# Fourier and mixture-of-experts kernel: sums of the right operands formed by adding DMAs, elementwise work moved from GpSimd to VectorE in the Fourier stage, one gate multiplied later

## The chip, the cores and the metric

One core of a Trainium2 chip runs the whole program. The metric is the device time of one execution in microseconds (us). Times of the profile come from one profiled execution, counted from its first instruction. PE is TensorE, PEld its weight loads, DVE is VectorE, ACT is ScalarE, POOL is GpSimd, SP is SyncE, which here only issues DMAs.

## The reference

For x of 2048 positions by 512 features, the output is g * a + (1 - g) * b, with one sigmoid gate g for each position:

```python
a_re = x @ dft_hid_re.T ; a_im = x @ dft_hid_im.T          # 512 x 512
a = dft_seq_re @ a_re - dft_seq_im @ a_im                  # 2048 x 2048
for e in range(8):                                         # all 8 experts, K = 8
    b += softmax(x @ w_gate)[:, e] * (silu(x @ w1[e]) @ w2[e])
g = sigmoid((x * gate_w).sum(-1))
out = g * a + (1 - g) * b
```

## The kernel before

Every large product is float32 made of two parts (a high part that ACT writes as fp32r, a low part that an elementwise engine gets by subtracting it), so one product of tiles is three matmuls (`mm`, lines 126 to 131). The products are arranged in blocks of 2 x 2 in a scheme of Strassen and Winograd with seven block products m = 1 to 7 in place of eight. It needs sums of blocks of each operand before the products and sums of products after them.

The program runs in this order. Stage 1 (`plan_stage1`) makes x times the hidden matrices, in two halves of positions (hf 0 and 1), seven products of 24 matmuls each, in the order `ORDER1`; `plan_x_op`, `plan_x_sums`, `plan_w_op`, `plan_w_sums` make its operands and `evict1` takes its results out of PSUM. Then come four phases of the sequence transform, in this order: X of output half 0, X of half 1, Y of half 1, Y of half 0 (below X0, X1, Y1, Y0). An X phase makes products 1, 2 and 5, a Y phase products 6, 3, 7 and 4, each over 16 steps k of the contraction (`dft`). One step is 18 matmuls of 512 columns in X and 24 in Y. The left operands of a step (tiles `xl`) are made once for both halves from the results of stage 1 (`raw`): for X by `plan_left_x`, for Y by `plan_left_y`, which loads the raw tile again from DRAM (`rawy`). The right operands are made anew in each step by `plan_right`: SP loads blocks of the sequence matrix (`cT`, tiles `ca`, `cb`, `cd`), sums are formed, and `wide` and `split_at` make the high and low parts (tiles c_kh, c_kl, from the pool `cp` of 9 buffers; the loads go to the pool `stage` of 6). In X one sum is made, d - a0, on DVE. In Y the first sum, b1 - b0, is made on POOL, and the next two, a0 and a1, on DVE. `plan_left_y` makes three sums and one low part on POOL and one low part on DVE for each k.

`plan_out_x` and `plan_out_y` take the sums out of PSUM at the end of a phase; Y1's four output tiles are multiplied by the gate row g on POOL and stored to DRAM (`yd`), Y0's are multiplied and stay on chip. Between the phases, `plan_logits` and `softmax` make the expert gates. Then 86 steps of the experts follow (43 pairs of chunks for each half of positions): `plan_ff1` with its activation and operands, `plan_ff2`, and the weights' operands by `plan_w1` and `plan_w2` on ACT and POOL. The results of half 1 are added onto `yd`, which `load_acc` brings back when half 0 is done.

The order of work is written out by hand: each `ev(t, ...)` gives a piece of work a planned time, all pieces are sorted by it, and each engine, and SP's DMA queue, takes its own pieces strictly in that order. A planned time is thus only a place in a queue: a piece that waits holds up all behind it on the same engine. The product slot is planned as SLOT = 2.72 us, a Y step as TY = 5.44, an X step as TX = 4.08 (4.55 in X0, where the logits come between). `base` shifts the times of the experts to the end of Y0.

Of the kernel before, what the change touches and what calls it, by code (L numbers as in the profile page):

```python
# [15 lines left out]
P = 128  # L16
# [34 lines left out]
def fnet_moe_kernel(ctx: ExitStack, tc: tile.TileContext, xT, cT, wd, w1d, w2d, w2s, wg, out):  # L51
# [81 lines left out]
    def split_at(t_hi, t_lo, new, src, eng, keep, sg=1.0):  # L133

        v = {}

        def hi():
            v["w"], v["s"] = new(), src()
            keep(v["w"])
            act(v["w"][:, 0], v["s"], scale=sg)  # L140

        def lo():
            if sg == 1.0:
                eng(v["w"][:, 1], v["s"], f32(v["w"][:, 0]), sub)
            else:
                pin(nc.vector.scalar_tensor_tensor(v["w"][:, 1], v["s"], sg, f32(v["w"][:, 0]),
                                                   OP.mult, sub))
# [95 lines left out]
    ORDER1 = (1, 2, 6, 5, 7, 3, 4)  # L243
# [18 lines left out]
    def plan_w_op(m, k, t, eng):  # L262
        r, i = lambda j: xw["r", k][:, j, :], lambda j: xw["i", k][:, j, :]
        of = {1: lambda: r(0), 2: lambda: r(1), 7: lambda: xw["q", k], 5: lambda: i(0),
              6: lambda: r(0), 3: lambda: r(1), 4: lambda: i(1)}
        split_at(t, t + 0.65, lambda: xp.tile([P, 2, GT], F32R, tag="x", name=f"wo{m}_{k}"),
                 of[m], eng, lambda w: wop.__setitem__((m, k), w), -1.0 if m in (4, 5, 6) else 1.0)

    def plan_w_sums(k, t, t3):
        r, i = lambda j: xw["r", k][:, j, :], lambda j: xw["i", k][:, j, :]  # L270

        def s7():
            xw["q", k] = tmp.tile([P, GT], F32, tag="c", name=f"wq{k}")
            vt(xw["q", k], r(0), i(0), add)

        ev(t, s7)
        ev(t + 0.6, lambda: vt(i(0), i(0), i(1), add))
        ev(t + 1.2, lambda: vt(r(0), i(0), r(0), add))
        ev(t3, lambda: vt(r(1), r(1), r(0), add))
# [85 lines left out]
    def plan_stage1(hf, H):  # L365
        for n, m in enumerate(ORDER1):
            t = H + n * TM
            if hf == 0 and n == 0:
                ev(t, first1)
            else:  # L370
                for j in range(4):
                    ev(t + j * TM / 4, product1, hf, n, j)
            for j in range(4):
                late = t + TM if hf == 0 and n == 0 else t + (j + 1) * TM / 4
                ev(late + 0.3 + 0.01 * j, evict1, hf, n, j)
            for k in range(2):
                if n < 2:
                    p = H + (-4.0 if n == 0 else 1.0) + 1.3 * k - (3 if hf else 0)
                else:
                    p = H + (n - 1) * TM - 1.0 + 2.2 * k  # L380
                plan_x_op(hf, m, k, p, pt if n else vt)
                ev(p + 3, store_x, hf, m, k)
                if m == 2:
                    q = H + 2.2 + 0.3 * k - (3 if hf else 0)
                    plan_x_op(hf, 8, k, q, pt)
                    ev(q + 4, store_x, hf, 8, k)
                    plan_x_sums(hf, k, q + 0.7, H + 5 * TM - 2.5, vt if hf == 0 else pt)
# [33 lines left out]
    def plan_left_y(k, s):  # L421

        v = {}

        def load():
            xraw[k] = xp.tile([P, 4, 256], F32, tag="x", name=f"rawy{k}")
            nc.sync.dma_start(xraw[k], rawd[k])

        def s3():
            v["q"] = tmp.tile([P, 2, 256], F32, tag="c", name=f"xs{k}_1")  # L430
            pt(v["q"][:, 0, :], xraw[k][:, 0, :], xraw[k][:, 1, :], sub)

        ev(s - 7, load)
        ev(s, s3)
        ev(s + 0.8, lambda: pt(v["q"][:, 1, :], xraw[k][:, 3, :], v["q"][:, 0, :], sub))
        ev(s + 1.6, lambda: pt(xraw[k][:, 2, :], xraw[k][:, 2, :], v["q"][:, 1, :], sub))
        left_pair(s + 1.7, s + 2.4, 7, 6, k, lambda: v["q"], pt)
        left_pair(s + 2.5, s + 3.2, 3, 4, k, lambda: xraw[k][:, 2:4, :], vt)
# [15 lines left out]
    def plan_right(pr, ph, k, t_load, t, r, eng=vt, lo=None):  # L454

# [3 lines left out]
        if ph == "X":  # L459
            def load():  # L460
                v["a"] = stage.tile([P, 2, GT], F32, tag="stage", name=f"ca{nm}")
                nc.sync.dma_start(v["a"], cT[pr, k][:, 0:2, :])
                v["d"] = tmp.tile([P, GT], F32, tag="c", name=f"cd{nm}")
                nc.sync.dma_start(v["d"], cT[pr, k][:, 2, :])

# [47 lines left out]
    def gate_y(hf, t, i, a, eng):  # L513
        eng(t, t, gy[hf][:, a, None, :].to_broadcast([P, 2, GT]), OP.mult)
        if hf:
            nc.sync.dma_start(yd[i, a], t)
        else:
            acc[hf, i, a] = t

    def plan_out_x(pr, te, ps):  # L520
# [30 lines left out]
    def plan_out_y(pr, te, ps):  # L551
# [16 lines left out]
        else:  # L568
            ev(te - 14, gate_y_row, 1, gp, "g")
        t = te - 2.1  # L570
        for n in range(2):
            ev(t + 0.69 * n, sum_, "s1", None, None, 6, n)
            ev(t + 1.38 + 0.69 * n, sum_, "c12", xp, "x", 3, n)
            ev(t + 2.76 + 0.69 * n, sum_, "s1", None, None, 7, n)
            ev(t + 4.14 + 0.69 * n, sum_, "c21", *((stage, "stage") if pr else (xp, "x")), 4, n)
        geng = pt if pr else vt
        ev(t + 7.5, lambda: vt(v["c12"], v["c12"], v["p5"], add))
        ev(t + 8.8, lambda: vt(v["p5"], v["p5"], v["s1"], add))
        ev(t + 9.0, lambda: gate_y(pr, v["c21"], 1, 0, geng))
        ev(t + 10.0, lambda: gate_y(pr, v["c12"], 0, 1, geng))  # L580
        ev(t + 11.0, lambda: gate_y(pr, v["p5"], 1, 1, geng))
# [35 lines left out]
    for pr, ph in phases:  # L617
        dt = TY if ph == "Y" else TX if pr else TX0
        ps = {}
        for k in range(NK):  # L620
            s, r = T + k * dt, {}
            t = s - (6.8 if ph == "X" else 8.3)
            if before == "Y" and k == 1:
                plan_right(pr, ph, k, t - 7, T - 4.0, r, pt, T - 2.1)
            else:
                if before == "Y" and k == 2:
                    t = T + 3.4
                plan_right(pr, ph, k, t - 7, t, r)
# [3 lines left out]
        if (pr, ph) == (1, "X"):  # L632
# [4 lines left out]
            for k in range(NK):  # L637
                plan_left_y(k, T - 4 + 9.2 * k)
# [119 lines left out]
    def plan_ff1(i):  # L758
# [3 lines left out]

        def product(n, key, m, start, stop):
# [181 lines left out]
```

## Time and profile before

| | |
|---|---|
| three runs, median (lowest to highest) | 2104.24 us (2103.17 to 2105.17) |
| the profiled execution, its own time | 2103.92 us |
| its span, first to last instruction | 2102.1 us |
| mean granted TensorE clock | 0.994 of 2.4 GHz |
| busy: PE, PEld, DVE, ACT, POOL | 2055.4, 1685.7, 1648.4, 1256.8, 1682.9 us |
| DMA moved | 241.45 MB, 115 GB/s in the mean |

Busy PE includes matmuls that overlap, so the time from start to start of a matmul says more than its length. A row of a table of stretches holds the stretch, its length, the busy time and count of instructions of each engine, the granted clock (1.00 is 2.4 GHz, 0.50 is 1.2 GHz), the busy share of the 16 DMA engines and what they moved in GB/s. In tables of waits each row has the total, the number and the longest.

### The profile page before, as it was taken

How to read it: one execution, taken by the hardware profiler on the slowest of the kernel's cores; microseconds unless marked ns; L12 is line 12 of the kernel's file. 1: busy time of each engine (PE TensorE's matmuls, PEld its weight loads, DVE VectorE, ACT ScalarE, POOL GpSimd, SP SyncE). 2: the span in 40 equal slices, each digit the busy share in tenths (PEclk: the TensorE clock that was granted, in tenths of full speed). 3: DMA queues.
4: the chain of work that ended last, by engine and by line, in shares of the span. 5: the costliest groups of instructions: out<-in, count | busy, mean ns of one | idle time of the engine just before them, and what ended most of it. 6: DMA issues, size and time to landing. Idle time of an engine off the chain costs nothing.

```text
span 2102.1 us, 26673 instructions
## 1 busy us (share of the span) xinstructions
PE 2055.4 (98%) x8984; PEld 1685.7 (80%) x8984; DVE 1648.4 (78%) x2356; ACT 1256.8 (60%) x2240; POOL 1682.9 (80%) x1507
## 2 busy tenths in 40 slices
PE   7999998989999999999999999999999999999998
PEld 6778776767888888888888888888888888888886
DVE  7777999878777777778777777777777777777777
ACT  5655443446666666666666666666666666666663
POOL 4624776378888889888888898888988888889884
PEclk9999999999999999999999999999999999999999
DMA  8897755942112121211221254112111212121111
GB/s 311 313 413 244 257 195 180 350 150 69 63 61 91 41 70 65 78 59 60 69 83 41 71 207 141 60 45 91 60 54 64 85 61 71 41 91 61 51 41 40
DMA packets 71970, 241.45 MB, mean 115 GB/s; under 512 B 8436, under 2 KB 8436, under 8 KB 71832
## 3 DMA queue, kind: packets, MB, share of 16 engines
q1 hardware_dynamic: 71832, 239.74, 32.8%
q8 instruction: 70, 1.15, 0.2%
q14 instruction: 68, 0.56, 0.1%
HBM read 206.61 MB, written 33.10 MB: 114 GB/s over the span
## 4 chain that ended last, share of the span: by engine, by line
PE 87%; POOL 3%; DVE 3%; issue 3%; DMA 2%; ACT 1%; SPq 0%; POOLq 0%; ACTq 0%; DVEq 0%
PE o_b L127 7%; PE o_b L131 7%; PE o_b L130 7%; PE m_b L127 7%; PE m_b L131 7%; PE m_b L130 7%; PE o_d L127 4%; PE o_d L131 4%; PE o_d L130 4%; PE m_d L127 4%; PE m_d L131 4%; PE m_d L130 4%; PE u L130 3%; PE u L131 3%; PE u L127 3%
## 5 line engine op out<-in xcount | busy, mean ns | idle before, releaser
L118 POOL TENSOR_TENSOR w<-w1s,w 128x512 fp32r<-128x512 f32 x258 | 334.8, 1298 | 146.4 <-ACT w L124 146.2
L118 POOL TENSOR_TENSOR w<-w2s,w 128x512 fp32r<-128x512 f32 (+1 forms) x264 | 335.0, 1269 | 37.3 <-ACT w L124 37.2
L127 PE MATMUL m_b<-xb,w 128*128 128x512 f32 x688 | 268.2, 390 | 6.3 <-ACT s L124 6.3
L127 PE MATMUL o_b<-h,w 128*128 128x512 f32 x688 | 268.4, 390 | 1.9 <-ACT h L124 1.4
L131 PE MATMUL o_b<-h,w 128*128 128x512 f32 x688 | 267.9, 389 | 0.0
L130 PE MATMUL o_b<-h,w 128*128 128x512 f32 x688 | 267.9, 389 | 0.0
L131 PE MATMUL m_b<-xb,w 128*128 128x512 f32 x688 | 267.8, 389 | 0.0
L130 PE MATMUL m_b<-xb,w 128*128 128x512 f32 x688 | 267.7, 389 | 0.0
L124 ACT ACTIVATE w<-w1s 128x512 fp32r<-128x512 f32 x258 | 162.0, 628 | 134.2 <-POOL w1s L118 134.1
L118 POOL TENSOR_TENSOR h<-b,h 128x512 fp32r<-128x512 f32 x172 | 223.4, 1299 | 4.7 <-ACT h L124 4.7
L124 ACT ACTIVATE h<-m_c 128x512 fp32r<-128x512 f32 x172 | 103.1, 600 | 191.3 <-DVE m_c L121 188.5
L118 POOL TENSOR_TENSOR w1s<-w1s 128x256 f32<-128x256 f32 x258 | 193.1, 749 | 6.8
L121 DVE TENSOR_TENSOR acc<-o_b,acc 128x512 f32<-128x512 f32 x176 | 121.4, 690 | 59.0 <-PE o_b L131 57.6
L124 ACT ACTIVATE h<-b 128x512 fp32r<-128x512 f32 x172 | 108.7, 632 | 93.2 <-PE m_d L131 57.9
L124 ACT ACTIVATE w<-w2s 128x512 fp32r<-128x512 f32 (+1 forms) x264 | 162.4, 616 | 2.6 <-POOL w2s L118 2.6
L127 PEld LDWEIGHTS m_b<-xb,w 128*128 128x128 f32 x688 | 129.1, 188 | 34.9 <-ACT s L124 8.2
L127 PEld LDWEIGHTS o_b<-h,w 128*128 128x128 f32 x688 | 129.2, 188 | 30.7 <-ACT h L124 1.8
L131 PEld LDWEIGHTS o_b<-h,w 128*128 128x128 f32 x688 | 129.3, 188 | 27.0
L131 PEld LDWEIGHTS m_b<-xb,w 128*128 128x128 f32 x688 | 129.1, 188 | 27.0
L130 PEld LDWEIGHTS o_b<-h,w 128*128 128x128 f32 x688 | 129.3, 188 | 26.6
L130 PEld LDWEIGHTS m_b<-xb,w 128*128 128x128 f32 x688 | 129.1, 188 | 26.6
L127 PE MATMUL m_d<-xb,w 128*128 128x512 f32 x344 | 133.9, 389 | 2.7 <-ACT p L124 2.7
(535 smaller groups left out, 5802.3 us busy)
## 6 DMA issues: line engine op xcount, KB each, us to landing
w1s<-w_dram SPq DMA_DIRECT2D x86, 512.0 KB, 3.3
w2s<-w_dram SPq DMA_DIRECT2D x84, 512.0 KB, 3.5
ca<-cT_dram SPq DMA_DIRECT2D x64, 512.0 KB, 7.8
xbd<-xo SPq DMA_DIRECT2D x32, 512.0 KB, 4.4
cb<-cT_dram SPq DMA_DIRECT2D x32, 512.0 KB, 5.7
xb<-xbd SPq DMA_DIRECT2D x28, 512.0 KB, 7.5
rawd<-raw SPq DMA_DIRECT2D x16, 512.0 KB, 7.1
cd<-cT_dram SPq DMA_DIRECT2D x32, 256.0 KB, 8.3
```

The source lines that it names most:

```text
L118: pin(nc.gpsimd.tensor_tensor(*a))
L121: pin(nc.vector.tensor_tensor(*a))
L124: pin(nc.scalar.activation(dst, src, f, **kw))
L127: ins = nc.tensor.matmul(ps, lh, rh, start=start, stop=False, skip_group_check=True)
L130: nc.tensor.matmul(ps, lh, rl, start=False, stop=False, skip_group_check=True)
L131: nc.tensor.matmul(ps, ll, rh, start=False, stop=stop, skip_group_check=True)
```

## The change

1. **Right operands.** In `plan_right` the sum that combined two loaded blocks is no longer an instruction of DVE (X) or POOL (Y). One block is loaded first, and a DMA issued from POOL's queue with `accum_op=add` adds the other block from DRAM onto it in SBUF. The block that takes part in another sum is still loaded by SP as before, so in each of the 64 steps one block of 256 KB is read once more. Signs are moved: the sum has a plus sign, and other sums and evictions take a minus in turn (`plan_w_sums`, `plan_out_x`, `c21`, a negated gate for the second quarters in `softmax_end`). `split_at` loses its factor of -1. The order of loads is `d` before `a` in X, `b` before `a` in Y, planned 1 us earlier.
2. **No GpSimd elementwise in the Fourier stage.** `plan_x_op`, `plan_x_sums`, `plan_left_x` and `plan_left_y` run on DVE where POOL ran them. `plan_left_y` starts 8 us earlier and runs every 6.5 us, where it was 9.2.
3. **Other product order.** `ORDER1` is (1, 2, 5, 6, 7, 3, 4); it was (1, 2, 6, 5, 7, 3, 4). The operands of the second product are planned 2 us earlier, ahead of the sums.
4. **Evictions of Y.** The sums are planned 2.3 us earlier, product 4 is copied out by ACT, and the last sums of Y1 come 12 us later, inside Y0.
5. **Half 1 gated inside the experts.** Y1's and X1's outputs are stored ungated. `plan_gate_late` loads each of the four tiles and the gate row back to two `stage` buffers during the experts' steps 6, 10, 14 and 18, multiplies on POOL and stores.
6. **Seam to the experts.** Times of the experts start 8.5 us earlier (OFF); those of the first step, which has no second product beside it, are compressed to about half. The operands x of the experts are loaded over a longer stretch of Y0.

The core of the diff:

```diff
-    ORDER1 = (1, 2, 6, 5, 7, 3, 4)
+    ORDER1 = (1, 2, 5, 6, 7, 3, 4)
...
-            vt(xw["q", k], r(0), i(0), add)
+            vt(xw["q", k], r(0), i(0), sub)
...
-                    p = H + (-4.0 if n == 0 else 1.0) + 1.3 * k - (3 if hf else 0)
+                    p = H + (-4.0 if n == 0 else -1.0) + 1.3 * k - (3 if hf else 0)
...
-                plan_x_op(hf, m, k, p, pt if n else vt)
+                plan_x_op(hf, m, k, p, vt)
...
-            pt(v["q"][:, 0, :], xraw[k][:, 0, :], xraw[k][:, 1, :], sub)
+            vt(v["q"][:, 0, :], xraw[k][:, 0, :], xraw[k][:, 1, :], sub)
...
-        left_pair(s + 1.7, s + 2.4, 7, 6, k, lambda: v["q"], pt)
+        left_pair(s + 1.7, s + 2.4, 7, 6, k, lambda: v["q"], vt)
...
-                nc.sync.dma_start(v["a"], cT[pr, k][:, 0:2, :])
                 v["d"] = tmp.tile([P, GT], F32, tag="c", name=f"cd{nm}")
                 nc.sync.dma_start(v["d"], cT[pr, k][:, 2, :])
+                nc.sync.dma_start(v["a"], cT[pr, k][:, 0:2, :])
+
+            def more():
+                pin(nc.gpsimd.dma_start(v["d"], cT[pr, k][:, 0, :], accum_op=add))
...
-            ev(t, lambda: vt(v["d"], v["d"], v["a"][:, 0, :], sub))
-            wide(t - 0.5, lo, lambda: v["a"], eng, keep, f"c12{nm}")
+            ev(t_load + 0.5, more)
+            wide(t - 0.5, lo, lambda: v["a"], vt, keep, f"c12{nm}")
...
+        def more():
+            pin(nc.gpsimd.dma_start(v["b"][:, 0, :], cT[pr, k][:, 3, :], accum_op=add))
...
-        ev(t - 0.6, lambda: pt(v["b"][:, 0, :], v["b"][:, 1, :], v["b"][:, 0, :], sub))
+        ev(t_load + 0.5, more)
...
-            ev(te + 2, lambda: gate_y(1, v["c11"], 0, 0, pt))
...
-        t = te - 2.1
...
+            ev(te - 4.4 + 0.69 * n, sum_, "s1", None, None, 6, n)
...
-        geng = pt if pr else vt
...
-            plan_left_x(8 + k, T1 + 0.9 + 4.4 * k, pt)
+            plan_left_x(8 + k, T1 + 0.9 + 4.4 * k, vt)
...
-                plan_left_y(k, T - 4 + 9.2 * k)
+                plan_left_y(k, T - 12 + 6.5 * k)
...
-    base[0] = T
+    OFF = 8.5
+    base[0] = T - OFF
...
+        def ev(t, fn, *args):
+            d = t - T
+            if i == 0:
+                d = OFF + (d / 2 if d < 13 else 6.5 + 0.95 * (d - 13))
+            ev_(T + d, fn, *args)
...
+    def plan_gate_late(i, a, t):
+        v = {}
+
+        def load():
+            for key in ("y", "g"):
+                v[key] = stage.tile([P, 2, GT], F32, tag="stage", name=f"late{key}{i}{a}")
+            nc.sync.dma_start(v["y"], yd[i, a])
+            gate_row(v["g"], slice(0, P), E, 1)
+
+        ev(t - 10, load)
+        ev(t, lambda: pt(v["y"], v["y"], v["g"][:, a, None, :].to_broadcast([P, 2, GT]), OP.mult))
+        ev(t + 2, lambda: nc.sync.dma_start(yd[i, a], v["y"]))
...
+    for n in range(4):
+        plan_gate_late(n // 2, n % 2, (4 * n + 6) * STEP + 0.5)
...
-        ev(-TY * (10 - n), load_x, 0, m)
+        ev(OFF - TY * (12.5 - 1.4 * n), load_x, 0, m)
```

## Rows read from the trace of the kernel before

**Rows 1.** The table of stretches, cut at the borders of the stages: stage 1 half 0, half 1, X0, X1, Y1, Y0 up to its step 4, Y0 from step 5 to 14, the experts' beginning, their long middle.

```profile
5.96:54.71 48.75, 42.88 (x169) 34.24 (x169) 36.36 (x48) 26.01 (x49) 22.31 (x16) 0.93 0.88 330
54.71:96.94 42.23, 40.32 (x169) 32.15 (x168) 30.80 (x40) 24.28 (x47) 30.82 (x23) 0.96 0.78 293
96.94:174.10 77.16, 77.16 (x354) 60.44 (x352) 53.17 (x60) 37.71 (x61) 22.78 (x20) 1.00 0.90 356
174.10:241.38 67.28, 67.28 (x305) 55.30 (x305) 62.02 (x64) 40.83 (x60) 37.71 (x31) 1.00 0.79 274
241.38:350.35 108.97, 95.26 (x385) 74.65 (x384) 102.47 (x77) 42.69 (x51) 78.56 (x50) 0.95 0.60 205
350.35:383.54 33.19, 29.82 (x121) 23.58 (x122) 31.50 (x27) 9.84 (x10) 19.38 (x10) 0.95 0.62 215
383.54:437.94 54.40, 54.40 (x242) 45.04 (x240) 43.33 (x39) 21.41 (x22) 23.06 (x16) 1.00 0.92 353
444.85:500.00 55.15, 46.18 (x192) 36.48 (x191) 47.54 (x70) 37.71 (x72) 44.95 (x46) 0.97 0.19 60
500.00:2050.00 1550.00, 1550.00 (x6839) 1283.27 (x6838) 1195.04 (x1870) 994.03 (x1830) 1372.62 (x1265) 1.00 0.22 71
```

**Rows 2.** PE's waits in Y1 (241 to 350.4 us), two of the longest.

```profile
PE u L127 <- DVE s L121: 2.4, 1, 2.4
PE u L130 <- DVE c_6l L121: 2.2, 1, 2.2
```

**Rows 3.** DVE's instructions in Y1, grouped by tile and shape: the busy time and the mean length in ns, then DVE's idle time ahead of them.

```profile
L121 DVE TENSOR_TENSOR ca<-ca 128x512 f32<-128x512 f32 x17 | 21.3, 1252 | 0.5
...
L121 DVE TENSOR_TENSOR c_12l<-ca,c_12h 128x1024 fp32r<-128x1024 f32 x1 | 2.3, 2317 | 0.0
...
L121 DVE TENSOR_TENSOR c_10l<-cb,c_10h 128x1024 fp32r<-128x1024 f32 x1 | 1.8, 1764 | 0.0
...
L121 DVE TENSOR_TENSOR c_0l<-cb,c_0h 128x1024 fp32r<-128x1024 f32 x1 | 1.2, 1220 | 0.0
```

**Rows 4.** POOL's instructions in Y1, grouped in the same way.

```profile
L118 POOL TENSOR_TENSOR cb<-cb 128x512 f32<-128x512 f32 x16 | 27.2, 1706 | 0.7 <-DMA cb<-cT_dram 0.6
...
L118 POOL TENSOR_TENSOR xs<-rawy 128x256 f32<-128x256 f32 x8 | 11.2, 1397 | 0.8 <-DMA rawy<-rawd 0.8
...
L118 POOL TENSOR_TENSOR c<-c,gy 128x1024 f32<-128x1024 f32 x1 | 3.3, 3306 | 1.2 <-DVE c L121 1.2
```

**Rows 5.** DVE in order of time in Y0 (386 to 401 us): start, length.

```profile
386.05 1.23 DVE L121 TENSOR_TENSOR c_6l<-ca,c_6h 128x1024 fp32r<-128x1024 f32 x1
387.19 0.68 DVE L121 TENSOR_TENSOR ca<-cb,ca 128x512 f32<-128x512 f32 x1
387.91 0.69 DVE L121 TENSOR_TENSOR ca<-ca 128x512 f32<-128x512 f32 x1
388.52 1.22 DVE L121 TENSOR_TENSOR c_7l<-cb,c_7h 128x1024 fp32r<-128x1024 f32 x1
```

**Rows 6.** PE in order of time at the start (13 to 27 us), with its idle time and what ended it.

```profile
14.05 0.39 PE L131 MATMUL s00a<-wo,xo 128*128 128x512 f32 x1
15.86 0.49 PE L127 MATMUL s00a<-wo,xo 128*128 128x512 f32 x1 [1.42 <-ACT wo L124]
20.30 0.80 PE L130 MATMUL s00a<-wo,xo 128*128 128x512 f32 x1 [3.95 <-DVE wo L121]
...
26.72 0.39 PE L127 MATMUL s00b<-wo,xo 128*128 128x512 f32 x1
```

**Rows 7.** DVE in the same stretch: a sum that ran beside a POOL instruction, and the low part that PE waited for behind the sums.

```profile
16.09 1.75 DVE L121 TENSOR_TENSOR wq<-wdr,wdi 128x512 f32<-128x512 f32 x1
...
18.96 0.68 DVE L121 TENSOR_TENSOR xa<-xa 128x512 f32<-128x512 f32 x1
19.57 0.68 DVE L121 TENSOR_TENSOR wo<-wdr,wo 128x512 fp32r<-128x512 f32 x1
```

**Rows 8.** PE's waits in half 1 of stage 1 (60 to 97 us).

```profile
PE s10b L131 <- POOL xo L118: 1.3, 2, 1.1
```

**Rows 9.** The DMA queues from 95 to 165 us: all packets, and one kind of issue with its count, size and median time from issue to landing.

```profile
DMA packets 8974, 27.71 MB, mean 396 GB/s; under 512 B 1004, under 2 KB 1004, under 8 KB 8969
...
cd<-cT_dram SPq DMA_DIRECT2D x18, 256.0 KB, 8.7
```

**Rows 10.** The same view from 36 to 50 us, where the queue is short.

```profile
xbd<-xo SPq DMA_DIRECT2D x6, 512.0 KB, 2.6
```

**Rows 11.** X0: DVE in order of time (126 to 140 us), with what it waited for, and PE's first matmul of step 8.

```profile
128.89 1.21 DVE L121 TENSOR_TENSOR c_8l<-ca,c_8h 128x1024 fp32r<-128x1024 f32 x1
...
138.20 0.69 DVE L121 TENSOR_TENSOR cd<-cd,ca 128x512 f32<-128x512 f32 x1 [3.72 <-DMA cd<-cT_dram]
```

**Rows 12.** PE in order of time, 134.2 to 134.6 us.

```profile
134.44 0.39 PE L127 MATMUL u<-c_8h,xl 128*128 128x512 f32 x1
```

**Rows 13.** The end of X0 as a stretch.

```profile
158.00:172.00 14.00, 14.00 (x63) 11.18 (x62) 6.70 (x8) 4.87 (x8) 3.13 (x3) 1.00 0.36 139
```

**Rows 14.** PE's waits at the beginning of the experts (444.5 to 500 us).

```profile
PE m_b L127 <- ACT s L124: 6.3, 4, 3.2
PE m_d L127 <- ACT p L124: 2.7, 1, 2.7
```

**Rows 15.** POOL's costliest group in the experts' middle (500 to 2050 us), with POOL's idle time ahead of it.

```profile
L118 POOL TENSOR_TENSOR w<-w1s,w 128x512 fp32r<-128x512 f32 x246 | 318.0, 1293 | 133.7 <-ACT w L124 133.6
```

More of the change, by code (lines that the diff above doesn't have):

```diff
@@ L131, in mm, with split_at @@
         nc.tensor.matmul(ps, ll, rh, start=False, stop=stop, skip_group_check=True)
-    def split_at(t_hi, t_lo, new, src, eng, keep, sg=1.0):
+    def split_at(t_hi, t_lo, new, src, eng, keep, ev=ev):
         v = {}
@@ L139, in hi @@
             keep(v["w"])
-            act(v["w"][:, 0], v["s"], scale=sg)
+            act(v["w"][:, 0], v["s"])
         def lo():
[L143 to L147, printed above, removed]
+            eng(v["w"][:, 1], v["s"], f32(v["w"][:, 0]), sub)
         ev(t_hi, hi)
@@ L219, in softmax_end @@
         vt(st[:, 2, :], st[:, 2, :], st[:, 1, :], OP.mult)
+        odd = g.rearrange("p (h a i) -> p h a i", h=2, a=2)[:, :, 1, :]
+        pin(nc.vector.tensor_scalar(odd, odd, -1.0, None, OP.mult))
         vt(e_, e_, st[:, 2, :][:, :, None].to_broadcast([P, NS, E]), OP.mult)
@@ L266, in plan_w_op @@
         split_at(t, t + 0.65, lambda: xp.tile([P, 2, GT], F32R, tag="x", name=f"wo{m}_{k}"),
-                 of[m], eng, lambda w: wop.__setitem__((m, k), w), -1.0 if m in (4, 5, 6) else 1.0)
+                 of[m], eng, lambda w: wop.__setitem__((m, k), w))
     def plan_w_sums(k, t, t3):
@@ L384, in plan_stage1 @@
                     q = H + 2.2 + 0.3 * k - (3 if hf else 0)
-                    plan_x_op(hf, 8, k, q, pt)
+                    plan_x_op(hf, 8, k, q, vt)
                     ev(q + 4, store_x, hf, 8, k)
-                    plan_x_sums(hf, k, q + 0.7, H + 5 * TM - 2.5, vt if hf == 0 else pt)
+                    plan_x_sums(hf, k, q + 0.7, H + 5 * TM - 2.5, vt)
                 if hf == 0:
@@ L514, in gate_y @@
         eng(t, t, gy[hf][:, a, None, :].to_broadcast([P, 2, GT]), OP.mult)
[L515 to L518, printed above, removed]
+        acc[hf, i, a] = t
     def plan_out_x(pr, te, ps):
@@ L527, in snap @@
                 v[key] = pool.tile([P, 2, GT], F32, tag=tag, name=f"{key}{pr}")
-            act(v[key][:, n, :], ps[m, n])
+            act(v[key][:, n, :], ps[m, n], scale=-1.0 if m == 5 else 1.0)
             if pr == 0 and n == 1:
@@ L534, in c11 @@
                 v["c11"] = stage.tile([P, 2, GT], F32, tag="stage", name=f"c11{pr}")
-            vt(v["c11"][:, n, :], ps[2, n], v["s1"][:, n, :], add)
-            if n == 1 and pr == 0:
-                nc.sync.dma_start(sd[2], v["c11"])
+            vt(v["c11"][:, n, :], v["s1"][:, n, :], ps[2, n], sub)
+            if n == 1:
+                nc.sync.dma_start(yd[0, 0] if pr else sd[2], v["c11"])
         for n in range(2):
@@ L567, in plan_out_y, with c21 @@
             ev(te - 22, lambda: gate_y(0, v["c11"], 0, 0, pt))
-        else:
-            ev(te - 14, gate_y_row, 1, gp, "g")
-        t = te - 2.1
-        for n in range(2):
[L572 to L575, printed above, removed]
-        geng = pt if pr else vt
[L577 to L581, printed above, removed]
+        def c21(n):
+            if n == 0:
+                v["c21"] = (stage if pr else xp).tile([P, 2, GT], F32, tag="stage" if pr else "x",
+                                                      name=f"c21{pr}")
+            act(v["c21"][:, n, :], ps[4, n])
+        for n in range(2):
+            ev(te - 4.4 + 0.69 * n, sum_, "s1", None, None, 6, n)
+            ev(te - 3.0 + 0.69 * n, sum_, "c12", xp, "x", 3, n)
+            ev(te - 1.6 + 0.69 * n, sum_, "s1", None, None, 7, n)
+            ev(te - 0.3 + 0.6 * n, c21, n)
+        d = 12 if pr else 0
+        for n, (key, b, o, i, a) in enumerate((("c21", "s1", sub, 1, 0), ("c12", "p5", add, 0, 1),
+                                               ("p5", "s1", add, 1, 1))):
+            if o == sub:
+                ev(te + 1 + d, lambda: vt(v["c21"], v["s1"], v["c21"], sub))
+            else:
+                ev(te + 2.2 + 1.3 * n + d, lambda key=key, b=b: vt(v[key], v[key], v[b], add))
+            if pr:
+                ev(te + 3.5 + 1.3 * n + d, lambda key=key, i=i, a=a: nc.sync.dma_start(yd[i, a], v[key]))
+            else:
+                ev(te + 5 + 1.5 * n, lambda key=key, i=i, a=a: gate_y(0, v[key], i, a, vt))
     acc, xbs, gy = {}, {}, {}
@@ L622, in fnet_moe_kernel @@
             t = s - (6.8 if ph == "X" else 8.3)
[L623 to L628, printed above, removed]
+            if before == "Y" and k in (1, 2):
+                t = T + (-0.4, 3.4)[k - 1]
+            plan_right(pr, ph, k, t - 8, t, r)
             ev(s, dft, pr, k, (1, 2, 5) if ph == "X" else (6, 3, 7, 4), r, ps)
```

32 lines of the change are left out of this document (13 added, 19 removed).

## The prediction

> **What bounds the kernel now.** I read the table of stretches first, then PE's waits in the stretches that lose time, then the engine that ended those waits. The table [rows 1] gives the pace that PE can keep: from 383.54 to 437.94 us it runs ten Y steps of 24 matmuls without idling, so a matmul costs 54.40 / 240 = 0.2267 us and a Y step 5.44. By that pace each half of stage 1 (168 matmuls) is worth 38.1 us, a Y phase 87.0. In the middle of the experts PE is busy for all 1550 us, so there is nothing to gain there, and the whole case lies in the first 500 us. The losses [rows 1]: half 0 takes 48.75 (10.7 over), half 1 takes 42.23 (4.1 over), X0 and X1 show no idle PE, Y1 takes 108.97 (21.9 over), the first five steps of Y0 take 33.19 for 27.2 (6.0 over), its last step, from 437.94 to the next row's 444.85, is 1.5 over, and the experts' beginning has 55.15 - 46.18 = 9.0 us of idle PE. In the stretches that wait, the granted clock is 0.93 to 0.97 in the mean, so part of a loss is PE at 1.2 GHz after an idle time; it goes with the waits.
>
> In Y1 PE waits for DVE's low parts and sums [rows 2], and DVE is busy for 102.47 of 108.97 us: it is the bound there. But its instructions are not all of one length: the same 128x1024 subtraction takes 1.22, 1.76 or 2.32 us [rows 3], and POOL's ops are long too [rows 4]. Where nothing runs beside it, DVE keeps the short value [rows 5]. So DVE loses time to POOL's simultaneous work, and Y1 is slow from contention as much as from work. Y0's ten clean steps, where the left operands are already made, show the rest: PE is the bound there though POOL still makes one sum a step.
>
> **Part by part.** Work on DVE is counted by its spacing where nothing disturbs it [rows 5]: 387.91 to 388.52 is 0.61 us for 128x512, 386.05 to 387.19 is 1.14 for 128x1024. A 128x256 is estimated at half the work of 128x512, about 0.35.
>
> *Y phases.* DVE's list per step stays: two sums and two low parts, 2 x 0.61 + 2 x 1.14 = 3.50 us of 5.44. POOL's sum becomes a DMA. `plan_left_y` puts three 128x256 sums and one more low part on DVE: 3 x 0.35 + 2 x 0.61 = 2.27 us per k, every 6.5 us, or 1.9 a step. While both run, from 12 us before X1's start for 16 x 6.5 us, so until some 27 us into Y1, DVE has 5.4 us in 5.44; after that 3.5. The first five steps may fall behind by about half a microsecond each for waits on ACT, which the lead of the low parts (planned 5 us ahead of the step) takes up. I leave 2.4 of Y1's 21.9: gain 19.5 (bounds 12 and 21.5). In Y0 the gate multiplies of Y1's tiles on POOL, 3.31 us [rows 4] each, go from it, the eviction that PE waited 2.4 us for at the seam [rows 2] is planned 2.3 us earlier, and the sums of Y1 move behind step 2. Of 7.5 I take 6.3 (3 to 7.5).
>
> *X1* was not idle: no gain. DVE there has 1.14 + 0.61 per 4.08 us and 2.27 per 6.5, together 78%. No cost; a step of cover is there if it slips.
>
> *Start.* PE waited from 14.05 to 20.30, first for ACT, then for a low part [rows 6] that stood on DVE behind six sums, two of them stretched to 1.75 by POOL [rows 7]. Moving the second product's operands ahead of the sums takes this wait away. What is late next: product 5 now comes directly after product 2 and needs four PSUM banks that product 2's evictions on DVE free; those stand behind all 12 sums and the low parts of product 5. Counting 0.61 each from the last landing (the second sum started at 16.09 [rows 7]), with two more low parts now on DVE, the first eviction ends near 24.4 us, so PE stands from about 19 to 24.4 instead, and finishes three products near 31 to 32; in the trace the third began at 26.72 [rows 6] and needs 5.4, so 32.2. Gain 1.5, bounds -2 and 4. In half 1 PE waited for POOL's low parts [rows 8] and then ran at the lower clock; on DVE they have short neighbours: gain 3.3 of 4.1 (1 to 4).
>
> *Adding DMAs.* 64 of them, each 256 KB read once more. POOL's adding DMA waits for the landing of its first block; queued behind it on POOL are only the next adding DMAs, so nothing else is held, but ACT's high part and DVE's sum wait for it in their order, and what follows on ACT, evictions too. Its latency is covered in Y, where loads run up to three steps (16 us) ahead; the trace does not show the operation itself. A plain 512 KB DMA into a short queue took 2.6 us to land [rows 10], a 256 KB one in a full queue 8.7 [rows 9]. What counts is the time that it holds the DMA engines. Lower bound: its own bytes, 262 KB at 396 GB/s [rows 9], 0.66 us (a gain is excluded, as bytes are only added). Upper bound: as long as the 512 KB DMA took alone, 2.6. From 95 to 165 us the engines move 27.71 MB at 396 GB/s [rows 9], which I take as full, and DVE stands idle for operands (3.72 us) [rows 11]. The lead is thin: step 8's low part ends at 130.10 [rows 11], PE takes it at 134.44 [rows 12], 4.3 us. By step 10 eleven additions stand ahead: at 0.66 that is 7.3 less 4.3 to 4.6 of lead, some 2 us lost; at 1.3 (source and destination both read) about 9, and then X1's engines, 79% busy [rows 1], have 20 us more and PE starts Y1 without a stock: 13 in all. Towards the end of X0 there is a hole (36% busy for 14 us) [rows 13] that takes the rest. I take 8, between the two, as the nearest row is a load of the same 256 KB but the destination must be read too; for the range 0 and 26 (at 2 us each). By the Trainium skill (DMA: Bandwidth & Descriptors, Anatomy of one DMA) such a DMA would take 2.0 us plus bytes / 436 GB/s, an estimate of 2.6 us here, mostly latency; by it this term would be 2 and the time 2073. The same page (Issuing engines are not separate DMA queues) speaks against the change: a DMA from POOL's queue runs on the same 16 engines, so it brings no bandwidth of its own; no row before shows a DMA from POOL.
>
> *Seam to the experts.* PE waits five times for ACT's copies out of PSUM [rows 14]; the compressed times put the second step's copy ahead of two high parts of the first. But the chain through DVE, ACT and the first step's gates stays, and in steps 1 and 2 PE asks for 14 slots in less than planned. Gain 2.2 of 9.0 (-2 to 6).
>
> *Half 1's gates.* Four POOL instructions of up to 3.31 us [rows 4] in the experts, with two loads, a store and two `stage` buffers each. POOL idles 133.7 us before one group alone there [rows 15], 1.6 a step, and its weights are planned a step ahead, so 3.3 us are made up in two steps. The DMA engines are 22% busy [rows 1]. SP's store waits for POOL with the next weights' load behind it, 13 us later by plan. Cost 0; without that cover 4 x 3.3 = 13. The earlier `rawy` loads pass X1's first operands in SP's queue and use the hole at X0's end. The negated gate is one small instruction in X1: 0.
>
> **Sum.** 1.5 + 3.3 + 19.5 + 6.3 + 2.2 = 32.8 gained, 8 lost: 2103.9 - 24.8 = 2079.1. The profiled execution's 2103.92 is 0.3 below the median of 2104.24: 2079 us to the nearest.
>
> **Rivals.**
> (a) *The adding DMAs are dear and the DMA engines become the bound: slower.* For it: the full engines in X0 [rows 9]; against it: it takes 2.1 us each, over three times the bytes' time. From there X0 loses about 18, X1 and Y1's start 10, Y0 with the experts' operands the rest, and the 32.8 are gone; at 2.6 each X0 loses 16 x 2.6 - 12 = 30, X1 25, the Y phases 5: 2104 - 33 + 60 = 2131. Chance 0.09.
> (b) *Dear, but less so* (1.5 to 2.1 us): 18 to 28 lost, 2089 to 2100. Chance 0.10.
> (c) *The contention stays in another form*: POOL's writing of descriptors holds DVE as its elementwise did, about 0.6 us each. Then Y1's first steps need 6.0 of 5.44 and the start is slower: 8 more, 2087. For it: POOL and DVE disturb each other [rows 3, 4]; against it: POOL's work falls from 78.56 us in Y1 to one DMA a step. The Trainium skill (SBUF — State Buffer, Who interferes with whom) says that a DVE op with two SBUF inputs takes only the shared read interface, and infers that writing descriptors needs the write one; by it this rival would not happen, and no row here shows either. Chance 0.07.
> (d) *The late gates stall the experts*, 3.3 us each: 2092. Against it: POOL's idle time [rows 15]. Chance 0.05.
> (e) *DVE, with all of stage 1 on it, becomes the bound there, and the seam gives nothing*: 7 less, 2086; within my own range.
>
> **How the numbers follow.** The forecast with (e) has 0.69, with a range of its own of 2066 to 2092. A difference of 0.2%, 4.2 us, is about what a measurement of this kernel can tell from no change. Faster by more than that (below 2100): 0.69 + 0.10 + 0.07 + 0.05, less 0.03 for ends that meet, 0.88; within it 0.03; slower 0.09, which is (a). The range goes from 2065 (all gains at their upper bounds, adding DMAs for nothing to 2 us) to 2100, the end of (b).
>
> **What would show it.** Right: Y1 near 90 us with DVE's 128x1024 at 1.22 throughout; Y0 near 88; no elementwise instruction of POOL before the experts' weights; the PE wait at 14 to 20 us gone and a new one near 19 to 24. X0 longer than 77 us, with DVE or ACT waiting for DMAs, shows the price of the adding DMAs. Wrong: DVE still at 1.8 or 2.3 in Y1, waits of the first experts' steps longer than before, new waits of PE after 500 us.

## The result: 0.8% slower, and the profile after

The changed kernel takes 2120.84 us (median of four runs, 2119.06 to 2123.47) against 2103.71 us beside it: a ratio of 1.0081, 95% interval 1.0064 to 1.0099. The profiled execution took 2119.06 us, with a span of 2117.3.

The table of stretches of the changed kernel, cut at PE's first matmul of each stage: stage 1 half 0, half 1, X0, X1, Y1, Y0, the experts' beginning and middle. Columns as in [rows 1].

```profile
5.88:52.66 46.78, 41.68 (x168) 33.92 (x169) 38.03 (x63) 26.73 (x50) 0.00 (x0) 0.96 0.98 359
52.66:90.74 38.08, 38.08 (x169) 31.54 (x168) 33.08 (x59) 23.62 (x45) 1.88 (x2) 1.00 0.91 324
90.74:176.96 86.22, 80.94 (x353) 60.98 (x351) 41.42 (x61) 35.57 (x59) 15.22 (x18) 0.96 1.05 358
176.96:255.96 79.00, 69.90 (x305) 54.59 (x304) 56.50 (x94) 44.32 (x66) 13.87 (x16) 1.00 1.00 312
255.96:352.04 96.08, 91.67 (x384) 72.69 (x385) 75.06 (x96) 41.71 (x47) 14.37 (x17) 0.98 0.87 248
352.04:460.21 108.17, 94.61 (x386) 75.47 (x384) 73.62 (x72) 35.93 (x39) 31.53 (x29) 0.94 0.89 295
460.21:511.01 50.80, 41.60 (x176) 31.93 (x174) 43.90 (x63) 33.59 (x66) 38.75 (x38) 1.00 0.19 63
511.01:2050.00 1538.99, 1538.99 (x6789) 1274.22 (x6790) 1188.42 (x1860) 988.20 (x1820) 1374.14 (x1261) 1.00 0.23 76
```

Against [rows 1], half 0 is 2.0 us shorter, half 1 is 4.2 and Y1 12.9. X0 is 9.1 us longer, X1 11.7, and Y0, which took 94.50 us (350.35 to 444.85), 13.7. From Y0's end to the end of the span it is 1657.1 us, where it was 1657.3. The losses lie in the stages where the new transfers run, and in both X phases the share of the DMA engines is now 1.00 or more (0.90 and 0.79 before), while the rate went from 356 to 358 GB/s in X0 and from 274 to 312 in X1. A share over 1.00 (1.05 in X0) shows that the times of packets overlap, so a price worked out from shares is a near value.

The DMA queues in X1 of the changed kernel (packets, MB, share of 16 engines; then one kind of issue). q0 is the queue of the adding DMAs.

```profile
q1 hardware_dynamic: 6539, 20.33, 69.0%
q0 software_dynamic: 2344, 4.28, 31.1%
...
cd<-cT_dram POOLq DMA_DIRECT2D x14, 256.0 KB, 7.4
```

31.1% of 79.00 us, by 4.28 MB at 0.262 MB each (16.3 transfers), is 1.50 us of all 16 engines for one; and each lands 7.4 us after its issue. The waits of X0, of X1 and of Y0, each the total, the number and the longest:

```profile
ACT c L124 <- DMA cd<-cT_dram: 48.4, 15, 6.0
DVE c L121 <- ACT c L124: 36.5, 12, 5.4
...
PE lt L173 <- DMA xr<-xbd: 4.1, 2, 2.9
```

```profile
PE u L127 <- ACT s L124: 2.5, 2, 1.5
PE u L130 <- DVE c_12l L121: 1.7, 1, 1.7
```

```profile
DVE ca L121 <- DMA cb<-cT_dram: 27.8, 9, 8.6
```

In X ACT's high part of product 5 waits for the sum, and DVE's low part behind it; [rows 11] had 3.72 us of such a wait at one step. PE's own waits show how that becomes lost time. In X0, 4.1 of its 5.3 us of idle time were for the logits' loads (`xr`), which have nothing to do with the sums: they land 11.5 us after their issue in the median, 8.9 in the kernel without the sums (e1 below), and after this wait PE ran at the lower clock (0.57 in the mean from 115 to 123 us). So the full engines delayed loads that have no part in the sums. In X1 it waited for copies out of PSUM on ACT and for low parts on DVE that stand in these queues behind product 5's high or low part. In Y0 DVE's next sum waits. One step of Y0 in order of time:

```profile
377.40 1.03 SPq L483 DMA_DIRECT2D cb<-cT_dram  x1
...
385.67 0.86 POOL L486 DMA_DIRECT2D cb<-cT_dram  x1 [10.84 <-DVE c_6l L121]
...
393.58 0.69 DVE L121 TENSOR_TENSOR ca<-cb,ca 128x512 f32<-128x512 f32 x1 [8.55 <-DMA cb<-cT_dram]
...
396.17 0.33 SPq L483 DMA_DIRECT2D cb<-cT_dram  x1
...
396.28 0.79 PE L127 MATMUL u<-c_7h,xl 128*128 128x512 f32 x1 [3.98 <-ACT c_7h L124]
```

Step 7's block is loaded from 377.40, the addition is issued at 385.67 and DVE gets the sum at 393.58: 16.2 us for two transfers, one after the other. PE idles 4 us and then runs at the lower clock (1.2 GHz; 0.57 in the mean from 395 to 403 us).

What was moved off POOL did what it should. DVE in Y1, by tile and shape [rows 3]: the 128x1024 low parts, and the sums that took 1252 ns.

```profile
L121 DVE TENSOR_TENSOR ca<-ca 128x512 f32<-128x512 f32 x16 | 11.1, 691 | 0.4
...
L121 DVE TENSOR_TENSOR c_12l<-ca,c_12h 128x1024 fp32r<-128x1024 f32 x1 | 1.2, 1225 | 0.1
```

The start, PE in order of time; the wait at 14 to 20 us [rows 6] is gone and another one stands where product 5 needs its banks; the three first products are done at 30.90 us. And the late gates among POOL's groups in the experts' middle.

```profile
23.97 0.79 PE L127 MATMUL s00d<-wo,xo 128*128 128x512 f32 x1 [5.10 <-DVE raw L121]
...
30.90 0.39 PE L127 MATMUL s00b<-wo,xo 128*128 128x512 f32 x1
```

```profile
L118 POOL TENSOR_TENSOR latey<-latey,lateg 128x1024 f32<-128x1024 f32 x4 | 9.6, 2404 | 0.0
```

### The profile page after: what moved, and what is told of

Read it like the earlier page. It is cut to its first block, busy times and chain, and to the rows that moved or that the text cites. A ratio compares the mean times of both kernels' runs of the same rounds, so it can differ in the third digit from the quotient of the medians.

```text
span 2117.3 us, 26730 instructions
## 1 busy us (share of the span) xinstructions
PE 2058.5 (97%) x8984; PEld 1683.7 (80%) x8984; DVE 1600.7 (76%) x2441; ACT 1260.8 (60%) x2244; POOL 1528.1 (72%) x1421
## 4 chain that ended last, share of the span: by engine, by line
PE 80%; DVE 3%; DMA 3%; issue 1%; ACT 1%; SPq 0%; POOL 0%; DVEq 0%; POOLq 0%; ACTq 0%
PE o_b L127 7%; PE o_b L130 7%; PE o_b L131 7%; PE m_b L127 7%; PE m_b L130 7%; PE m_b L131 7%; PE o_d L127 4%; PE o_d L131 4%; PE o_d L130 4%; PE m_d L127 4%; PE m_d L130 4%; PE m_d L131 4%; DMA cb<-cT_dram 3%; PE o_a L127 2%; PE o_a L131 2%; PE o_a L130 2%
## 5 line engine op out<-in xcount | busy, mean ns | idle before, releaser
L464 POOL DMA_DIRECT2D cd<-cT_dram x32 | 28.0, 875 | 212.2 <-DVE xb L121 77.4
## 6 DMA issues: line engine op xcount, KB each, us to landing
cd<-cT_dram SPq DMA_DIRECT2D x32, 256.0 KB, 10.8
```

Of the source, the lines that this page charges most:

```text
L464: pin(nc.gpsimd.dma_start(v["d"], cT[pr, k][:, 0, :], accum_op=add))
```

## The experiments

**Length of each stage** (us), from the tables of stretches, with time and ratio to the kernel before (95% interval). "End" is from PE's first matmul of the experts to the end of the span. All variants but e8 start from the changed kernel. The stages are those of the one profiled execution, the time is the median; in e3 the profiled execution was 3 us over it.

| kernel | half 0 | half 1 | X0 | X1 | Y1 | Y0 | end | time | ratio |
|---|---|---|---|---|---|---|---|---|---|
| before | 48.8 | 42.2 | 77.2 | 67.3 | 109.0 | 94.5 | 1657.3 | 2103.7 to 2104.2 | 1 |
| after | 46.8 | 38.1 | 86.2 | 79.0 | 96.1 | 108.2 | 1657.1 | 2120.84 | 1.0081 (1.0064 to 1.0099) |
| e1 no sum | 47.8 | 38.1 | 77.2 | 67.3 | 87.0 | 87.9 | 1656.8 | 2070.09 | 0.9839 (0.9825 to 0.9854) |
| e2 sum on DVE | 47.0 | 38.1 | 77.2 | 68.0 | 89.7 | 88.2 | 1656.8 | 2073.09 | 0.9850 (0.9834 to 0.9866) |
| e3 plain copy | 48.4 | 38.1 | 78.8 | 70.8 | 91.5 | 101.9 | 1657.4 | 2091.56 | 0.9939 (0.9919 to 0.9959) |
| e8 before, with adding DMAs | 48.1 | 41.3 | 94.0 | 81.5 | 111.9 | 111.9 | 1657.8 | 2154.29 | 1.0243 (1.0227 to 1.0259) |
| e4 adding in Y alone | 47.5 | 38.1 | 77.2 | 67.3 | 90.8 | 106.3 | 1657.5 | 2092.79 | 0.9944 (0.9929 to 0.9959) |
| e5 adding in X alone | 46.9 | 38.1 | 85.0 | 78.9 | 93.5 | 88.2 | 1657.6 | 2096.41 | 0.9966 (0.9952 to 0.9980) |
| 7 stage buffers | 48.0 | 38.1 | 86.1 | 79.4 | 93.8 | 103.5 | 1657.6 | 2114.26 | 1.0052 (1.0037 to 1.0067) |
| 5 stage buffers | 46.5 | 38.1 | 85.6 | 79.2 | 99.0 | 122.7 | 1657.5 | 2136.09 | 1.0149 (1.0134 to 1.0165) |
| e9 two half DMAs | 47.9 | 38.1 | 89.2 | 85.9 | 94.6 | 109.4 | 1658.2 | 2133.01 | 1.0134 (1.0114 to 1.0154) |
| e10 half the columns | 46.7 | 38.1 | 78.9 | 73.0 | 93.0 | 102.5 | 1657.8 | 2095.69 | 0.9949 (0.9931 to 0.9968) |
| e11 left operands on POOL | 47.9 | 38.1 | 77.2 | 70.5 | 96.8 | 88.0 | 1657.2 | 2083.55 | 0.9899 (0.9884 to 0.9914) |
| e7 Y's sum on POOL | 47.8 | 38.1 | 77.2 | 67.7 | 95.4 | 91.3 | 1657.4 | 2081.85 | 0.9893 (0.9879 to 0.9908) |

**Is it the adding DMAs?** The theory was yes (A), with rivals that the rest of the change had failed (B, C). First without the 64 sums, then with the sum as one DVE instruction, which is the whole computation again.

```diff
-            ev(t_load + 0.5, more)
...
-        ev(t_load + 0.5, more)
```

> The changed kernel without its 64 adding DMAs: the block that they add stays unadded, so this leaves that part of the sums out. Theory A (the adding DMAs cost all that went wrong): the Fourier stage is bound by PE, about 2071 us, X0 near 77, Y0 near 88. Rival B (the changed order, the earlier raw loads or VectorE's longer list cost it): 2095 or more, with X0 and X1 still long.

```diff
-            ev(t_load + 0.5, more)
+            ev(t, lambda: vt(v["d"], v["d"], v["a"][:, 0, :], add))
...
-        ev(t_load + 0.5, more)
+        ev(t - 0.6, lambda: vt(v["b"][:, 0, :], v["b"][:, 0, :], v["b"][:, 1, :], add))
```

> The changed kernel with each of the 64 sums as one VectorE instruction of 0.61 us on blocks that are loaded anyway. Theory A: 2074, since X has room for it and only the first five steps of Y1 (6.0 us of work in 5.44) lose some 3 us. Rival C (wherever the sum goes, it is late: VectorE becomes the bound): 2090 or more, with PE waiting for low parts through all of Y1.

Both came out as A says, within 1 us. X0, X1, Y1 and Y0 without the sum, the table of stretches:

```profile
91.88:169.04 77.16, 77.16 (x354) 60.46 (x352) 44.52 (x68) 37.66 (x62) 0.00 (x0) 1.00 0.90 358
169.04:236.32 67.28, 67.28 (x305) 55.32 (x305) 56.64 (x96) 43.99 (x65) 0.00 (x0) 1.00 0.85 301
236.32:323.36 87.04, 87.04 (x385) 72.08 (x384) 71.94 (x91) 38.35 (x42) 0.00 (x0) 1.00 0.64 218
323.36:411.30 87.94, 87.34 (x386) 72.01 (x385) 69.53 (x69) 35.65 (x39) 19.66 (x15) 1.00 0.86 316
```

PE is never idle in the first three. The other way round, the kernel before with nothing but the adding DMAs:

```diff
-            ev(t, lambda: vt(v["d"], v["d"], v["a"][:, 0, :], sub))
+            ev(t_load + 0.5, lambda: pin(nc.gpsimd.dma_start(v["d"], cT[pr, k][:, 0, :], accum_op=add)))
...
-        ev(t - 0.6, lambda: pt(v["b"][:, 0, :], v["b"][:, 1, :], v["b"][:, 0, :], sub))
+        ev(t_load + 0.5, lambda: pin(nc.gpsimd.dma_start(v["b"][:, 0, :], cT[pr, k][:, 3, :], accum_op=add)))
```

> The kernel before with the adding DMAs alone (in X in place of VectorE's sum, in Y in place of GpSimd's), the signs of these sums left as they come out. Theory A: slower than before by what X0, X1 and Y0 lost, less GpSimd's op in Y1: 2110 to 2125. Rival B (they hurt only with the rest of the change): 2104 or less.

It costs 50 us there, more than I expected, and as much as between e1 and the changed kernel (2117.3 - 2068.1 = 49 us of span). That the totals agree is in part luck: X0 and X1 lose 16.8 and 14.2 us here and 9.1 and 11.7 there, and in this kernel the loads are neither reordered nor planned earlier, and the signs of the sums are not adapted. What it shows is that the transfers are dear without the rest of the change too.

**The addition, or a second transfer as such?** The same bytes, queue, place and waits, as a plain copy: the sum is replaced by the second block.

```diff
-                pin(nc.gpsimd.dma_start(v["d"], cT[pr, k][:, 0, :], accum_op=add))
+                pin(nc.gpsimd.dma_start(v["d"], cT[pr, k][:, 0, :]))
...
```

> The changed kernel with a plain DMA from GpSimd's queue in place of each adding one, same bytes, same place, same waits; the sum is replaced by the second block. Theory A1 (the time on the DMA engines is that of the addition): engines no longer full in X1, about 2080. Theory A2 (a second DMA in the chain and its 7 us to land, whatever it does): as the changed kernel, 2115 to 2122.

2091.56 lies between the two: neither is right alone. In X the copy costs 1.6 and 3.6 us where the addition cost 9.1 and 11.7; in Y0 it costs 14.0 of 20.2. The two phases thus suffer from different things. The following runs take them apart.

**By phase.** An addition in Y alone (first diff line of e2) and in X alone (second).

> The X phases form their sum by a DVE instruction, the Y phases keep their 32 adding DMAs. Theory P (each phase pays for its own adding DMAs): X0 and X1 take 77.2 and about 68 us, Y0 stays near 108 for its own round trip of load, addition and use, and Y1 falls from 96.1 to 89 to 92, since only its first steps were late: 2093 to 2097 us. Rival S (the lateness of the X phases is handed on, and the Y phases would keep pace if they began with a stock of operands): Y0 near 89 as well, 2075 to 2079 us.

> The Y phases form their sum by a DVE instruction, the X phases keep their 32 adding DMAs. Theory P: X0 and X1 stay at 86 and 79 us, Y1 takes 90 to 94 us, Y0 88: 2092 to 2097 us. Rival S (what is lost in X is handed on to Y): Y1 near 96 and Y0 over 95 also without additions, 2104 us or more.

Theory P holds in both (the first 0.2 us below its range), and S falls: each phase pays for its own. From the table, X's additions cost X0 and X1 19 to 21 us and Y1, at its first steps, some 4 to 5; Y's cost Y0 18 to 20 and Y1 1 to 3.

**What it is in Y0.** Each Y step holds two stage buffers from its loads to its last sum.

```diff
-    cp = ctx.enter_context(tc.tile_pool(name="cp", bufs=9))
-    stage = ctx.enter_context(tc.tile_pool(name="stage", bufs=6))
+    cp = ctx.enter_context(tc.tile_pool(name="cp", bufs=8))
+    stage = ctx.enter_context(tc.tile_pool(name="stage", bufs=7))
```

> The changed kernel with 7 stage buffers instead of 6, paid for by 8 buffers of high and low parts instead of 9. Theory L (in Y0 the steps in flight, two stage buffers each, are too few for the 20 us from load to release): 3.5 in place of 3 steps in flight, Y0 5 to 14 us shorter, 2106 to 2116 us. Rival O (the engine time of the additions is what fills Y0): no change beyond 3 us, 2118 to 2124 us.

> The changed kernel with 5 stage buffers instead of 6. Theory L: 2.5 steps in flight at some 20 us each are 8.1 us a step, so Y0 takes about 130 us (108 before), Y1 loses 10 to 17 us as well, and X little: 2145 to 2165 us. Rival O (the additions' time on the DMA engines is the bound): under 2128 us.

Y0 with 7 and with 5 buffers, the table of stretches:

```profile
351.25:454.73 103.48, 95.10 (x385) 75.44 (x384) 72.65 (x70) 36.13 (x39) 28.57 (x27) 0.93 0.90 303
```

```profile
354.83:477.54 122.71, 99.83 (x385) 77.40 (x385) 70.81 (x74) 36.12 (x39) 30.25 (x29) 0.90 0.83 261
```

103.5, 108.2 and 122.7 us for 7, 6 and 5 buffers: Theory L, though weaker than I expected at both ends (4.7 us gained for 5 to 14, Y0 122.7 for 130, and Y1 lost only 2.9; the 2136.09 us with 5 buffers lie between the two ranges). Step 7 above shows the working: its buffer is loaded from 377.40 and next at 396.17, so it is held for 18.8 us, and three steps in flight allow a step every 6.3 us where PE needs 5.44. The kernel with 7 buffers also has one buffer of high and low parts less, so it is not a clean test; the one with 5 changes nothing else. With 5 buffers the engines are less busy (0.83) and the phase is longer, which an engine bound can't give.

The engines have a part in it all the same. In Y0 they are idle for 0.14 x 87.94 = 12.3 us without the sums (e1); q0 takes 0.192 x 108.17 = 20.8 us of them with the additions and 0.106 x 101.9 = 10.8 with the plain copy:

```profile
q0 software_dynamic: 2016, 3.67, 19.2%
```

```profile
q0 software_dynamic: 1040, 3.41, 10.6%
```

By this ledger (what the transfers take, less the idle time) the copy would cost nothing and the addition 8.5 us, where Y0 lost 14.0 and 20.2. So 14 us go with the second transfer in the chain, and the time on the engines is enough for the other 6, which no run isolates.

**What it is in X.** Per transfer or per byte? Each addition cut into two of half the columns, then only the first of the two.

```diff
-                pin(nc.gpsimd.dma_start(v["d"], cT[pr, k][:, 0, :], accum_op=add))
+                pin(nc.gpsimd.dma_start(v["d"][:, 0:256], cT[pr, k][:, 0, 0:256], accum_op=add))
+                pin(nc.gpsimd.dma_start(v["d"][:, 256:512], cT[pr, k][:, 0, 256:512], accum_op=add))
...
```

> The changed kernel with each adding DMA cut into two of 128x256 elements: the same bytes, twice the rows, of half the length. Theory R (the price lies in the rows, 128 of 2 KB each): the two together hold the DMA engines twice as long, about 2.9 us where one took 1.45, and X0 and X1 lose a further 16 x 1.45 = 23 us each: 2150 us or more. Rival V (the price lies in the bytes): 2117 to 2128 us.

> The changed kernel with each adding DMA cut to the first 256 of its 512 columns; that part of the sums is left out. Theory R (price by rows): it holds the engines nearly as long, X0 and X1 stay within 3 us of 86 and 79: 2112 to 2122 us. Rival V (price by bytes): half of 1.45 us, which X0 and X1 can nearly hide, so they fall to 78 to 80 and 69 to 73 us; Y0 keeps the landing of a second transfer and stays over 100: 2095 to 2106 us.

The rows of the POOL queue's DMAs in the whole execution (packets, MB, share of the span), first of the changed kernel, then with the plain copy, with two halves, with half the columns:

```profile
q0 software_dynamic: 9216, 16.78, 4.6%
```

```profile
q0 software_dynamic: 5120, 16.78, 2.5%
```

```profile
q0 software_dynamic: 18432, 16.79, 5.2%
```

```profile
q0 software_dynamic: 9216, 8.39, 2.6%
```

Share times span by 64 sums is 1.52, 0.82, 1.73 and 0.85 us of the engines for each sum. As many packets with half the bytes take 0.85 for 1.52, twice the packets with the same bytes 1.73: the price goes mostly with the bytes. R falls; the time with half the columns is V's, that with two halves lies 5 us above V's range, for which the extra packets (1.73 for 1.52 us a sum) are the likely cause.

X0 and X1 follow these prices. Without the sums (e1, above) their engines are idle for 0.10 x 77.16 + 0.15 x 67.28 = 17.8 us. 32 transfers at the price that each kernel shows within X (q0's share, worked out as above: copy 0.69, half 0.83, whole 1.46, two halves 1.68) less 17.8 would lose 4.3, 8.8, 28.9 and 36.0 us. X0 and X1 together lost 5.2, 7.5, 20.8 and 30.6. The two dear ones lie 5 to 8 us under the ledger; Y1 takes over a part (9.0 and 7.6 us longer than in e1, 4.4 and 6.0 with the cheap ones). The landing time can't be the cause: 7.3 and 7.4 us whole, 6.6 to 6.9 for a half, nearly the same where the loss is 7.5 and where it is 30.6.

**Was Y1 slow from contention or from work?** The kernel of e2, with the left operands' sums and one low part of `plan_left_y` back on POOL; then the changed kernel with X's sum on DVE and Y's on POOL.

```diff
-        left_pair(s + 1.7, s + 2.4, 7, 6, k, lambda: v["q"], vt)
+        left_pair(s + 1.7, s + 2.4, 7, 6, k, lambda: v["q"], pt)
...
```

> The kernel with the sums of the right operands on DVE (2073 us), but the three sums and the low part of plan_left_y back on POOL. Theory K (in the kernel before, Y1 was slow because POOL's instructions stretch DVE's): DVE's 128x1024 subtraction goes from 1.22 to 1.7 us or more in X1 and Y1, Y1 takes 95 to 105 us: 2079 to 2090 us. Rival W (it was slow because DVE had too much work, and POOL takes some from it here): Y1 at 87 to 89 us, 2070 to 2073 us.

> The changed kernel with the sum on DVE in X and on POOL in Y, no adding DMA. Theory K: the 32 sums on POOL (1.7 us each) stretch DVE's instructions beside them, which have 83 us of work in the 90 of Y1: Y1 92 to 98 us, Y0 88 to 91, 2075 to 2083 us. Rival W: DVE has 0.6 us less in each step, Y1 87 to 89 us: 2069 to 2073 us.

Theory K in both. With less to do (96 instructions, 110 in e2) DVE is busy for longer in Y1 (89.9 us, 83.2 in e2), and a low part beside POOL takes twice its 686 ns. Y1 of e2, then of the first of the two, the stretch and one group:

```profile
236.66:326.36 89.70, 88.52 (x386) 71.73 (x384) 83.20 (x110) 39.88 (x44) 0.00 (x0) 1.00 0.64 213
```

```profile
L121 DVE TENSOR_TENSOR xl<-rawy,xl 128x512 fp32r<-128x512 f32 x5 | 3.4, 686 | 0.0
```

```profile
239.52:336.27 96.75, 91.56 (x384) 72.75 (x385) 89.92 (x96) 41.45 (x47) 23.33 (x17) 0.98 0.61 201
```

```profile
L121 DVE TENSOR_TENSOR xl<-rawy,xl 128x512 fp32r<-128x512 f32 x5 | 7.2, 1443 | 0.0
```

The best whole version is e2: the change with its sums as DVE instructions, 1.5% faster than the kernel before (0.9834 to 0.9866).

## Why the prediction was wrong

The sum was 32.8 us gained and 8 lost. Without the additions the gain is 34.0 us of span (2102.1 - 2068.1), with the sum on DVE 30.8. The term that failed is "Adding DMAs": 8 us predicted, 49 measured. The seam's 2.2 us did not come either.

- *Half 0* (1.5): the twelve kernels with this start vary from 46.5 to 48.4 us, the two with the old one took 48.8 and 48.1. About 1 us; the wait at 24 us and the end of the third product at 30.9 (near 31 to 32 predicted, 32.2 before) came as predicted. The order alone was not tried, so its part in the stage stays open. *Half 1* (3.3): 4.2, all of the loss. *X1* (0): right, 67.3 in e1.
- *Y phases* (19.5 and 6.3): 21.9 and 6.6 without the sum, 19.3 and 6.3 with it on DVE. Contention with POOL was the reason, as e11 and e7 show. DVE reached 83.2 of 89.7 us busy in e2 and PE hardly noticed.
- *Seam* (2.2): the end is 1656.8 to 1658.2 us in all fourteen kernels, so at most 0.5 is gained. PE still idles for 50.80 - 41.60 = 9.2 us at the experts' beginning (9.0 in [rows 1]). The compressed times changed which waits there are, not their sum. That the chain through DVE, ACT and the gates sets it, which I had named and not priced, is not shown by a run.
- *Half 1's gates* (0): right. 2.4 us each, hidden in POOL's idle time; rival (d) falls.
- *Adding DMAs, the price* (0.66 and 1.3 us of the engines reckoned through, 8 us of loss taken between them, 2.6 as the bound): 1.5 by the queue's row, above both. A plain copy through the same queue took 0.82, near the lower bound, so the row of a plain load was a bound for moving the bytes only, and the addition nearly doubles it.
- *Adding DMAs, the X phases* (8 in all, 2 at 0.66 and 13 at 1.3): 20.8. The price was too low, and the book-keeping failed. I followed the lead of 4.3 us up to step 10 and then let "X1's engines, 79% busy" and the hole at X0's end [rows 13] take the rest. The plain ledger takes two shares of [rows 1], idle engines for 0.10 x 77.16 + 0.21 x 67.28 = 21.8 us: 32 x 1.3 - 21.8 = 19.8 us lost at my own upper price, 32 x 1.46 - 21.8 = 24.9 at the one measured in X. I also looked for the loss at product 5 alone, while PE's longest wait in X0 was for the logits' loads.
- *Adding DMAs, the Y phases* ("its latency is covered in Y, where loads run up to three steps (16 us) ahead"): this sentence is false. The loads are ahead by what the stage buffers allow, and a buffer is held through two transfers in series and its use. In Y0, where the experts' operands share the engines, the two alone take 16.2 us at step 7. It cost 20 us in Y0, 14 of them also with a plain copy.

Rival (a), "dear", asked for 2.1 us a transfer and a full loss in X; the price was lower, yet its loss of 28 us in X0, X1 and Y1's start nearly came (9.1 + 11.7 and some 4 to 5); Y0's loss, which it put down to the experts' operands, was largely waiting. Rival (b), 1.5 to 2.1 us a transfer with 18 to 28 us lost, had the price at its lower end; it fell short at 2089 to 2100 us because it too had nothing for the chain in Y0. Rival (c) falls: DVE's instructions keep 1.22 us beside POOL's 64 issues of 0.87 us. The Trainium skill (SBUF — State Buffer, Who interferes with whom) infers that the two need different interfaces of the ports they share, so that neither holds the other, and these lengths agree. By the fit of the Trainium skill (DMA: Bandwidth & Descriptors, Anatomy of one DMA) the transfer would take an estimated 2.6 us; here it landed after 7.0 to 7.5 us in the median, so the measurement decides against the fit where other transfers stand in the same engines. The same page of the Trainium skill (Issuing engines are not separate DMA queues) says that a DMA of any issuing engine runs on the same 16 engines. The trace agrees: in X1 q0's 31.1% and q1's 69.0% add up to one full set of engines.

Two sums of the prediction do not come out, and neither changes the forecast. All gains at their upper bounds are 43 us, so the lower end of the range is 2061 to 2063 and not 2065; and by rival (a)'s own rule X0 loses 16 x 2.1 - 12 = 22 us at 2.1 us a transfer and not 18.

## What to carry to other kernels

Before moving a sum into a DMA, set up the ledger of each stage: the idle time of the DMA engines there against the number of transfers times their price, at both bounds, and let no later stage take the rest unless it has its own idle time over. A transfer that waits for another lengthens the time for which its buffer is held; count buffers times step time against the whole chain, not against one landing. In a stage with full engines look at what PE waits for, since the load that comes late need not be the new one. And when an instruction of POOL runs beside DVE, ask what it costs DVE: here an instruction on DVE of 0.69 us was the cheapest sum of the three.

## What the hardware showed that I had not expected

- An adding DMA of 256 KB held the 16 engines for 1.5 us by the time of its packets, a copy of the same bytes from the same queue for 0.82 (144 and 80 packets).
- It landed 7.0 to 7.5 us after its issue (median) in X0, X1, Y1 and Y0 alike, and halving its columns shortened that only to 6.7 to 6.8 in X.
- The row at 385.67 above names DVE as what POOL waited for. It is inferred: that addition's first load has no landing record, and where there is one, as at 394.56 (landed at 393.89), the addition is issued 0.67 us behind it. So the landing of step 7's load is the likelier releaser at 385.67 too, which the trace can't show. A releaser that ended by chance at the same time is easily read as the cause.
